# The gated unit's second group: four column blocks moved ahead of the first group's last four

## The chip, the cores and the metric

The kernel runs on one core of a Trainium2 chip. The metric is the device time of one launch in microseconds, lower is better. The engines that the text names are PE (TensorE, matmuls), PEld (its weight loads), DVE (VectorE), ACT (ScalarE), POOL (GpSimd) and SP (SyncE, which issues most DMAs). A few tenths of a per cent lie between runs of one kernel.

## The reference

Three stages follow each other on 2304 tokens of width 512 (4 batches of 576 rows, 8 heads of 64):

```
q, k rotated by position; attn = softmax(q k^T / 8);  x = attn v            # per batch and head
e = argmax(x w_gate); y = gate * sigmoid(x w_og)[e] * (relu(x w1[e]) w2[e])  # one of 8 experts, inner width 1024
out = (sigmoid(y Wg) * (y Wv)) Wo                                            # gated unit, inner width 1536
```

The last line is the gated unit. Its three weights come as float64 and the rest as float32; the result must hold to float32.

## The kernel before, in words

**Split matmuls.** Every large matmul works on operands that are split in two, a high half rounded to TensorE's faster fp32r type (`hi`) and a low half with what is left (`lo`), and adds three products: high by high, high by low, low by high. A weight is split by one ScalarE copy (`hi`) and one VectorE subtraction (`lo`).

**Expert stage.** The tokens are sorted by expert and worked in fourteen columns, numbered by their place in the program: a pair column has 256 tokens, a single one 128. Each column has eight units, j = 0 to 7: four for the first expert matrix (`l1`), four for the second (`l2`). In each unit the kernel records that unit's matmuls and the weight split of the unit three places ahead (lines 764 to 776), which also asks for the next column's weights. Column 13 is the held one: its results are scattered to `y_dram` during the gated unit (`put`, lines 868 to 875), in two scatters from POOL's queue.

**Conversion.** TensorE can't use float64, so `conv` (lines 948 to 973) makes a float32 piece from the two 32-bit halves of each number: ScalarE computes `mag` and `rnd`, VectorE the two steps of `sgn`, POOL the sum. There are 36 pieces of 128x512, one of each weight (gate `g`, value `v`, output `o`) for each of the twelve column blocks. Each needs a 512 KB load into one of three `cv` buffers (`conv_load`). Fifteen pieces are converted in the expert stage, at units 1 and 5 of pair columns and at unit 1 of single ones (line 913), from column 3 on. The other 21 are converted in the first group of the gated unit, two in each block (lines 1269 and 1270).

**Gated unit.** The tokens stand in six groups of 384 (`NG`), and the inner width in twelve column blocks of 128 (`NF`). The loop of lines 1263 to 1278 walks over the 72 pairs of group and block. One step records: the gate and value matmuls of this block (`gv`, 24 matmuls into the PSUM tiles `t` and `v`), the sigmoid on ScalarE, the product `gf` on VectorE and its two halves `gh` (ScalarE) and `gl` (POOL); the conversions that are due; the weight splits of the block two steps on (`wsplit`: `gh`, `gl`, `vh`, `vl`, `oh`, `ol`); and the output matmuls of the block before (`om`, 9 matmuls that add into three PSUM banks `o0` to `o2`). The three banks belong to one group at a time. After a group's twelfth block they are copied out (`ob`, two by ScalarE, one by VectorE) and stored. In four of a group's steps the next group's tokens, loaded by `load_y`, are transposed on TensorE and split (`ty`, its low half is `yl`).

Nothing reorders what is recorded: each engine and each DMA queue works in the order of the program, and waits at an instruction until its operands are there.

Of the kernel before, what the change touches and what calls it, by code (L numbers as in the profile page):

```python
# [9 lines left out]
F32 = mybir.dt.float32  # L10
F32R = mybir.dt.float32r
# [4 lines left out]
ALU = mybir.AluOpType  # L16
# [19 lines left out]
MAIN = list(range(NMAIN))  # L36
SPARES = (list(range(NMAIN, NCOL)),)
PAIRS = {*EARLY, *LATE_PAIRS}
HELD = MAIN[-1]
FRONT = 3  # L40
# [5 lines left out]
TG = 384  # L46
NG = NT // TG
KD = DM // 128
NF = FF // 128
# [3 lines left out]
NSPL = 4  # L53
CVB = 3
SCALE = D**-0.5
CONV_RATE = 2
CONV_AT = (1, 5)
TAIL = (3, 3, 0, 8, 9, 9, 9, 9, 9)
HI_EARLY = 6
NXG = 4  # L60
# [4 lines left out]
def tile_kernel(  # L65
# [16 lines left out]
    nc = tc.nc  # L82
    ctx.enter_context(tc.manual_schedule())

    def pool(stack, name, bufs, side="left", space=None):
        kw = {} if space is None else {"space": space}
        return stack.enter_context(tc.tile_pool(name=name, bufs=bufs, side=side, reuse_waits="tile", **kw))
# [622 lines left out]
    M = {}  # L710
# [14 lines left out]
    def tiles(s):  # L725
        return 2 if s in PAIRS else 1
# [9 lines left out]
    def more_ids():  # L736
        while M["ids"] < min(M["want"], len(M["seq"])):
            load_ids(M["seq"][M["ids"]])
            M["ids"] += 1
# [123 lines left out]
    def scale_y(s):  # L863
        for i in range(tiles(s)):
            ysb[s, i] = y = yp.tile([128, 512], F32, tag="ysb", name="ysb")
            nc.vector.tensor_scalar(out=y, in0=yps[s][i], scalar1=sc[s, i], scalar2=None, op0=ALU.mult)
# [10 lines left out]
    def moe_units(seq):  # L877

        m = len(seq)
        order = [(s, j) for s in seq for j in range(NPC)]  # L880
        nsp = [0]

        def ahead(upto):
            while nsp[0] < min(upto, len(order)):
                split(*order[nsp[0]])
                nsp[0] += 1

        yield lambda: ahead(1)
        yield lambda: ahead(2)
        yield lambda: (ahead(LOOK), tx(seq[0]))  # L890
        pos = 0
        for i, s in enumerate(seq):
            for j in range(NPC):
                pos += 1

                def unit(i=i, s=s, j=j, pos=pos):
                    (l1 if j < 4 else l2)(s, j)
                    ahead(pos + LOOK)
                    if j == 0 and i:
                        scale_y(seq[i - 1])  # L900
                        put(seq[i - 1], 0)
                        if M["table"]:
                            M["want"] = i + 4
                            more_ids()
                    if j == 4 and i:
                        put(seq[i - 1], 1)
                    if j == 1 and i + 2 < m and (seq is not MAIN or i + 2 != FRONT):
                        gather(seq[i + 2])
                    if s not in PAIRS and 1 <= j <= 4:
                        th(s, j - 1)  # L910
                    if j == 5 and i + 1 < m:
                        tx(seq[i + 1])
                    if seq is MAIN and FRONT <= i < m - 1 and j in CONV_AT[: tiles(s)]:
                        conv()

                yield unit
# [5 lines left out]
    CONV = [(f, n) for f in range(NF) for n in "gvo"]  # L922
    cl, cd = [0], [0]
# [117 lines left out]
    for t in range(NJ * NPAIR):  # L1041
        g, j = divmod(t, NJ)
# [33 lines left out]
        n = g + 2  # L1076
# [83 lines left out]
    moe_s.close()  # L1160


    ysp = pool(ctx, "ysp", 4, "right")
    wsp = [pool(ctx, "wsp0", 1, "right")]
    ytp = pool(ctx, "ytp", 2, "right")
    wsp += [pool(ctx, f"wsp{i}", 1, "right") for i in (1, 2)]
    osp = pool(ctx, "osp", 3, "right")
    gsp = pool(ctx, "gsp", 3, "right")
    NTT = TG // 128
    ytok, yT, ws, gs, ops_ = {}, {}, {}, {}, {}  # L1170

# [2 lines left out]
    def load_y(gr):  # L1174
        ytok[gr] = []
        for t in range(NTT):
            y = ysp.tile([128, DM], F32, tag="yt", name="yt")
            r0 = GROUPS[gr] * TG + t * 128 + 1
            nc.sync.dma_start(out=y, in_=y_dram[r0 : r0 + 128, :])
            ytok[gr].append(y)  # L1180

    def ty(gr, kk):
        if kk == 0:
            yT[gr] = (
                ytp.tile([128, KD, TG], F32R, tag="yh", name="yh"),
                ytp.tile([128, KD, TG], F32R, tag="yl", name="yl"),
            )
        ps = pst.tile([128, 512], F32, tag="t", name="t")
        for t in range(NTT):
            nc.tensor.transpose(ps[:, 128 * t : 128 * t + 128], ytok[gr][t][:, 128 * kk : 128 * kk + 128], idf)  # L1190
        hi, lo = (t[:, kk, :] for t in yT[gr])
        nc.scalar.copy(out=hi, in_=ps[:, 0:TG])
        nc.vector.tensor_tensor(out=lo, in0=ps[:, 0:TG], in1=hi.bitcast(F32), op=ALU.subtract)

    def wsplit(i):
        f = i % NF
        r = []
        gw, vw, ow = M["gw"], M["vw"], M["ow"]
        to = {nm: [wsp[i % 3].tile([128, 512], F32R, tag=nm + x, name=nm + x) for x in "hl"] for nm in "gvo"}
        for nm, t in (("g", gw[:, :, 128 * f : 128 * f + 128]), ("v", vw[:, :, 128 * f : 128 * f + 128]), ("o", ow[:, f, :])):  # L1200
            hi, lo = to[nm]
            shp = (lambda a: a) if nm == "o" else (lambda a: a.rearrange("p (k f) -> p k f", k=KD))
            nc.scalar.copy(out=shp(hi), in_=t)  # L1203
            nc.vector.tensor_tensor(out=shp(lo), in0=t, in1=shp(hi.bitcast(F32)), op=ALU.subtract)  # L1204
            r.append((hi, lo))
        ws[i] = r

    def gv(gr, f):
        i = gr * NF + f
        yh, yl = yT[gr]  # L1210
        pg = pst.tile([128, 512], F32, tag="t", name="t")
        pv_ = psv.tile([128, 512], F32, tag="v", name="v")
        for ps, (wh, wl) in ((pg, ws[i][0]), (pv_, ws[i][1])):
            for kk in range(KD):
                c = slice(128 * kk, 128 * kk + 128)
                nc.tensor.matmul(ps[:, 0:TG], wh[:, c], yh[:, kk, :], start=(kk == 0), stop=False)  # L1216
                nc.tensor.matmul(ps[:, 0:TG], wh[:, c], yl[:, kk, :], start=False, stop=False)  # L1217
                nc.tensor.matmul(ps[:, 0:TG], wl[:, c], yh[:, kk, :], start=False, stop=(kk == KD - 1))  # L1218
        sg = gsp.tile([128, TG], F32, tag="sg", name="sg")
        nc.scalar.activation(out=sg, in_=pg[:, 0:TG], func=AF.Sigmoid)  # L1220
        gf = gsp.tile([128, TG], F32, tag="gf", name="gf")
        nc.vector.tensor_tensor(out=gf, in0=pv_[:, 0:TG], in1=sg, op=ALU.mult)  # L1222
        gh = gsp.tile([128, TG], F32R, tag="gh", name="gh")
        gl = gsp.tile([128, TG], F32R, tag="gl", name="gl")
        nc.scalar.copy(out=gh, in_=gf)  # L1225
        nc.gpsimd.tensor_tensor(out=gl, in0=gf, in1=gh.bitcast(F32), op=ALU.subtract)  # L1226
        gs[i] = (gh, gl)

    def om(gr, f):
        i = gr * NF + f  # L1230
        if f == 0:
            ops_[gr] = [pso2.tile([128, 512], F32, tag=f"o{t}", name=f"o{t}") for t in range(NTT)]
        gh, gl = gs.pop(i)
        wh, wl = ws.pop(i)[2]
        for t in range(NTT):
            ps = ops_[gr][t]
            c = slice(128 * t, 128 * t + 128)
            nc.tensor.matmul(ps, gh[:, c], wh, start=(f == 0), stop=False)  # L1238
            nc.tensor.matmul(ps, gh[:, c], wl, start=False, stop=False)  # L1239
            nc.tensor.matmul(ps, gl[:, c], wh, start=False, stop=(f == NF - 1))  # L1240
        if f == NF - 1:
            for t in range(NTT):
                o = osp.tile([128, 512], F32, tag="ob", name="ob")
                (nc.vector.tensor_copy if t % 2 else nc.scalar.copy)(o, ops_[gr][t])
                r0 = GROUPS[gr] * TG + t * 128
                nc.sync.dma_start(out=out[r0 : r0 + 128, :], in_=o)

    N = NG * NF
    cd0 = cd[0]
# [10 lines left out]
    psv = pool(ctx, "psv", 2, "right", PSUM)  # L1260
    pso2 = pool(ctx, "pso2", 1, "right", PSUM)
    wsplit(1)
    for i in range(N + 1):
        gr, f = divmod(i, NF)
        if i < N:
            if f == 2 and gr + 1 < NG:
                load_y(gr + 1)
            gv(gr, f)
            while cd[0] < min(len(CONV), max(3 * (i + 3), cd0 + CONV_RATE * (i + 1))):
                conv()  # L1270
            if i + 2 < N:
                wsplit(i + 2)
        if i == 1:
            put(HELD, 1)
        if i >= 1:
            om(*divmod(i - 1, NF))
        if i < N and f >= 7 and f < 11 and gr + 1 < NG:
            ty(gr + 1, f - 7)


def _consts():
# [60 lines left out]
```

## Time and profile before

| | us |
|---|---|
| median of 3 runs | 1140.25 (1137.76 to 1144.18) |
| the profiled execution | 1140.11 |
| its span, first to last instruction | 1138.3 |
| PE busy | 1074.3 (94%) |
| DVE busy | 771.9 (68%) |
| ACT busy | 583.7 (51%) |
| POOL busy | 353.1 (31%) |

The span is what the profiler saw between the first and the last instruction; the execution's own time is 1.8 us more. Attention ends and the experts begin at about 430 us, the gated unit's first matmul starts at 658.85 us. A busy share is an average over these three stages. TensorE's granted clock was 1.00 of full speed in every stretch of the expert stage and the gated unit.

In a row of a timeline the first number is the start in us from the span's start, the second the duration. Instructions of one engine overlap a little at their ends, and a matmul's recorded duration (0.33 us) is longer than the distance to the next one.

### The profile page before, as it was taken

To read this page: it belongs to the slowest core of one execution; us is meant where nothing else is said; L and a number is where in the kernel's file an instruction comes from. 1 tells how busy PE (TensorE), PEld (TensorE's weight loads), DVE (VectorE), ACT (ScalarE), POOL (GpSimd) and SP (SyncE) were. 2 spreads that over 40 slices of the span, in tenths; PEclk is the share of its full clock that TensorE was granted. 3 is DMA by queue.
4 is the path that set the end of the run, shared out by engine and by line. 5 is a ranking of instruction groups with operands and counts; after the bars stand their busy time and mean duration, and the time that the engine had idled before them with its cause. 6 is when DMAs were issued, how large, how long until landed. Compare 5 with 4: busy or idle time off the path is not lost. (4 is left out here: it accounts for less than half of the span.)

```text
span 1138.3 us, 20687 instructions
## 1 busy us (share of the span) xinstructions
PE 1074.3 (94%) x7682; PEld 958.8 (84%) x7682; DVE 771.9 (68%) x1439; ACT 583.7 (51%) x1122; POOL 353.1 (31%) x336
## 2 busy tenths in 40 slices
PE   7799989999988999999999998889999999999998
PEld 6688778878867988888988887689999999999997
DVE  5778787878776886888888778864454444545442
ACT  3456555546554345567567555644443444444442
POOL 6335554654612104333233044521111111111111
PEclk8899999999999999999999999999999999999999
DMA  4134045025008296698999435310010010100000
GB/s 111 37 73 86 7 54 92 19 53 97 21 22 223 46 188 234 210 307 286 308 305 308 148 102 186 112 56 1 1 56 1 1 56 1 56 1 2 28 1 28
DMA packets 97053, 111.61 MB, mean 98 GB/s; under 512 B 16817, under 2 KB 75441, under 8 KB 96946
## 3 DMA queue, kind: packets, MB, share of 16 engines
q1 hardware_dynamic: 92482, 97.81, 30.6%
q0 software_dynamic: 4320, 12.08, 3.6%
q8 instruction: 62, 1.02, 0.4%
q14 instruction: 45, 0.37, 0.1%
q10 hardware_dynamic: 144, 0.33, 0.1%
HBM read 103.03 MB, written 15.56 MB: 104 GB/s over the span
## 5 line engine op out<-in xcount | busy, mean ns | idle before, releaser
L1226 POOL TENSOR_TENSOR gl<-gf,gh 128x384 fp32r<-128x384 f32 x72 | 73.4, 1019 | 349.4 <-ACT gh L1225 349.4
L291 ACT ACTIVATE p<-s,nm 128x576 f32<-128x576 f32 x144 | 105.6, 738 | 123.8 <-DVE nm L284 123.8
L770 DVE TENSOR_TENSOR lo<-wr,hi 128x1024 fp32r<-128x1024 f32 x112 | 150.4, 1359 | 16.8 <-ACT hi L769 15.8
L1222 DVE TENSOR_TENSOR gf<-v,sg 128x384 f32<-128x384 f32 x72 | 40.0, 555 | 136.7 <-PE v L1218 136.7
L284 DVE TENSOR_REDUCE nm<-s 128x1 f32<-128x576 f32 x144 | 102.8, 751 | 38.4 <-PE s L278 25.1
L1204 DVE TENSOR_TENSOR gl<-gw,gh 128x512 fp32r<-128x512 f32 x72 | 73.8, 1025 | 68.9 <-ACT gh L1203 68.9
L1225 ACT CAST gh<-gf 128x384 fp32r<-128x384 f32 x72 | 36.9, 513 | 162.1 <-DVE gf L1222 162.1
L769 ACT CAST hi<-wr 128x1024 fp32r<-128x1024 f32 x106 | 109.5, 1051 | 3.6 <-PE y L860 2.7
L1216 PE MATMUL t<-yh,gh 128*128 128x384 f32 x288 | 98.8, 343 | 9.2 <-ACT sg L1220 8.3
L324 PE MATMUL t<-idf,p 128*128 128x128 f32 x576 | 84.5, 281 | 21.2 <-DVE pt L310 17.6
L1218 PE MATMUL t<-yh,gl 128*128 128x384 f32 x288 | 97.5, 339 | 4.2 <-DVE gl L1204 4.2
L1217 PE MATMUL t<-yl,gh 128*128 128x384 f32 x288 | 96.6, 336 | 0.0
L327 ACT COPY pt<-t 128x512 f32<-128x512 f32 x144 | 79.5, 589 | 33.2 <-PE t L324 26.4
L1216 PE MATMUL v<-yh,vh 128*128 128x384 f32 x288 | 96.2, 334 | 0.0
L1217 PE MATMUL v<-yl,vh 128*128 128x384 f32 x288 | 96.2, 334 | 0.0
L1218 PE MATMUL v<-yh,vl 128*128 128x384 f32 x288 | 96.2, 334 | 0.0
L324 PEld LDWEIGHTS t<-idf,p 128*128 128x128 f32 x576 | 66.6, 145 | 28.2 <-DVE pt L310 22.9
L1240 PE MATMUL o<-oh,gl 128*128 128x512 f32 x216 | 86.2, 399 | 0.2 <-POOL gl L1226 0.2
L1239 PE MATMUL o<-ol,gh 128*128 128x512 f32 x216 | 85.3, 395 | 0.0
L1238 PE MATMUL o<-oh,gh 128*128 128x512 f32 x216 | 84.0, 389 | 0.0
L829 PE MATMUL h<-xh,hi 128*128 128x256 f32 x288 | 82.0, 285 | 1.9 <-DVE hl L834 1.9
L829 PE MATMUL h<-xl,hi 128*128 128x256 f32 x288 | 82.0, 285 | 1.6 <-DVE sc L805 1.6
(227 smaller groups left out, 2900.0 us busy)
## 6 DMA issues: line engine op xcount, KB each, us to landing
wr<-in_moe_w_dram SPq DMA_DIRECT2D x112, 512.0 KB
cv<-in_moe_w_gate_dram SPq DMA_DIRECT2D x12, 512.0 KB
cv<-in_moe_w_val_dram SPq DMA_DIRECT2D x12, 512.0 KB
cv<-in_moe_w_out_dram SPq DMA_DIRECT2D x12, 512.0 KB
yt<-y_dram SPq DMA_DIRECT2D x18, 256.0 KB
out_dram<-ob SPq DMA_DIRECT2D x18, 256.0 KB
kraw<-in_k_dram SPq DMA_DIRECT2D x16, 256.0 KB
qraw<-in_q_dram SPq DMA_DIRECT2D x16, 256.0 KB
```

The source lines that it names most:

```text
L284: nc.vector.tensor_reduce(out=nm, in_=s[:, :, 0:288], axis=AX.XY, op=ALU.max, negate=True)
L291: nc.scalar.activation(out=P[g, j][:, e, :].rearrange("p (a b) -> p a b", a=2), in_=s[:, :, 0:288], func=AF.Exp, bias=nm, scale=1.0, accum ...
L324: nc.tensor.transpose(ps[:, 128 * c : 128 * c + 128], src[:, e, k0 + 128 * c : k0 + 128 * c + 128], idf)
L769: nc.scalar.copy(out=hi, in_=t)
L770: nc.vector.tensor_tensor(out=lo, in0=t, in1=hi.bitcast(F32), op=ALU.subtract)
L829: nc.tensor.matmul(ps[:, c, :], w[:, kk, 128 * c : 128 * c + 128], x[:, kk, :], start=first, stop=last)
L1216: nc.tensor.matmul(ps[:, 0:TG], wh[:, c], yh[:, kk, :], start=(kk == 0), stop=False)
L1217: nc.tensor.matmul(ps[:, 0:TG], wh[:, c], yl[:, kk, :], start=False, stop=False)
L1218: nc.tensor.matmul(ps[:, 0:TG], wl[:, c], yh[:, kk, :], start=False, stop=(kk == KD - 1))
L1238: nc.tensor.matmul(ps, gh[:, c], wh, start=(f == 0), stop=False)
L1239: nc.tensor.matmul(ps, gh[:, c], wl, start=False, stop=False)
L1240: nc.tensor.matmul(ps, gl[:, c], wh, start=False, stop=(f == NF - 1))
```

## The change

The loop of the gated unit now follows a list, `ORDER`: blocks 0 to 7 of the first group, blocks 0 to 3 of the second, blocks 8 to 11 of the first, blocks 4 to 11 of the second, then the other groups as before. Since the three banks hold the first group's sums until its last block, the output matmuls of the second group's first eight blocks are put off (the table `AFTER`): they follow from step 16 on, two in a step until they have caught up. The products of the four early blocks wait in a pool of their own (`ghd`). The output weights of the second group's blocks 0 to 7 are not split with their gate and value weights but by `late_w`, two output blocks ahead, into the tiles that the conversion used (`mag` and `rnd` of the pool `cvt`).

Pair columns of the expert stage get a third conversion, at unit 3 (`CONV_AT`), so that 20 pieces are done by its end and 16 are left. These are spread over twelve steps by the table `CONV_BY`. The second group's tokens are loaded at step 0 and transposed in steps 3 to 6. The pool `ysp` has three buffers instead of four, `sg` and `gf` have two instead of three.

```diff
-CONV_RATE = 2
-CONV_AT = (1, 5)
+CONV_BY = (1, 3, 4, 6, 7, 9, 10, 12, 13, 14, 15, 16)
+ND = 4
+CONV_AT = (1, 3, 5)
...
-                    if seq is MAIN and FRONT <= i < m - 1 and j in CONV_AT[: tiles(s)]:
+                    if seq is MAIN and FRONT <= i < m - 1 and j in CONV_AT[: 3 if s in PAIRS else 1]:
                         conv()
...
+    LATE, LATE_O = ([(1, f) for f in range(n)] for n in (ND, 2 * ND))
+    ORDER = [(0, f) for f in range(NF - ND)] + LATE
+    ORDER += [(0, f) for f in range(NF - ND, NF)] + [(1, f) for f in range(ND, NF)]
+    ORDER += [(gr, f) for gr in range(2, NG) for f in range(NF)]
+    AFTER = {i: [] for i in range(len(ORDER) + 1)}
+    for i, x in enumerate(ORDER):
+        if x[0] != 1:
+            AFTER[i + 1].append(x)
+    for f in range(NF):
+        AFTER[NF + ND + (f + 1) // 2 if f < 2 * ND else NF + f + 1].append((1, f))
...
     def wsplit(i):
+        gr, f = ORDER[i]
+        ws[gr, f] = [wsplit_one(wsp[i % 3], nm, f) for nm in ("gv" if (gr, f) in LATE_O else "gvo")]
...
-        wh, wl = ws.pop(i)[2]
+        wh, wl = wod_[i] if i in LATE_O else ws.pop(i)[2]
...
+    def late_w(f):
+        wod_[1, f] = wsplit_one(M["cvt"], "o", f, ("mag", "rnd"))
+
     for i in range(N + 1):
-        gr, f = divmod(i, NF)
         if i < N:
-            if f == 2 and gr + 1 < NG:
+            gr, f = ORDER[i]
+            if i == 0:
+                load_y(1)
+            elif f == 2 and 1 <= gr < NG - 1:
                 load_y(gr + 1)
             gv(gr, f)
-            while cd[0] < min(len(CONV), max(3 * (i + 3), cd0 + CONV_RATE * (i + 1))):
+            ready = 3 * (ORDER[min(i + 3, N - 1)][1] + 1)
+            while cd[0] < min(len(CONV), max(ready, cd0 + CONV_BY[min(i, len(CONV_BY) - 1)])):
                 conv()
             if i + 2 < N:
                 wsplit(i + 2)
         if i == 1:
             put(HELD, 1)
-        if i >= 1:
-            om(*divmod(i - 1, NF))
-        if i < N and f >= 7 and f < 11 and gr + 1 < NG:
-            ty(gr + 1, f - 7)
+        for x in AFTER[i]:
+            om(*x)
+            if x in LATE_O[:-2]:
+                late_w(x[1] + 2)
+        if i in (NF, NF + 2):
+            late_w((i - NF) // 2)
+        if i < N:
+            if gr == 0 and 3 <= f < 7:
+                ty(1, f - 3)
+            elif 1 <= gr < NG - 1 and 7 <= f < 11:
+                ty(gr + 1, f - 7)
```

Where the instructions now stand, at three places. In a row, the first names are the tile written and the tiles read. Line numbers of the changed kernel differ from those before.

On VectorE, in the gated unit's first group, a step before the change (step 2) begins with the product of its block and has two conversions (four rows of `sgn`) ahead of three weight splits:

```order
L1222 TENSOR_TENSOR gf<-v,sg 128x384
L961 TENSOR_SCALAR sgn<-cv 128x512
L962 SCALAR_TENSOR_TENSOR sgn<-mag,sgn 128x512
L961 TENSOR_SCALAR sgn<-cv 128x512
L962 SCALAR_TENSOR_TENSOR sgn<-mag,sgn 128x512
L1204 TENSOR_TENSOR gl<-gw,gh 128x512
L1204 TENSOR_TENSOR vl<-vw,vh 128x512
L1204 TENSOR_TENSOR ol<-ow,oh 128x512
```

Steps 8 and 9 after the change, the first two of the second group's early blocks:

```order
L1237 TENSOR_TENSOR gf<-v,sg 128x384
L962 TENSOR_SCALAR sgn<-cv 128x512
L963 SCALAR_TENSOR_TENSOR sgn<-mag,sgn 128x512
L1216 TENSOR_TENSOR gl<-gw,gh 128x512
L1216 TENSOR_TENSOR vl<-vw,vh 128x512
L1237 TENSOR_TENSOR gf<-v,sg 128x384
L962 TENSOR_SCALAR sgn<-cv 128x512
L963 SCALAR_TENSOR_TENSOR sgn<-mag,sgn 128x512
L1216 TENSOR_TENSOR gl<-gw,gh 128x512
L1216 TENSOR_TENSOR vl<-vw,vh 128x512
```

One conversion stands in each of these steps, and no split of output weights.

On VectorE in the expert stage, a pair column from its second unit to the end of its sixth, before the change (`hl` is the low half of the hidden values, `lo` that of a weight piece, `xl` that of the next column's tokens):

```order
L770 TENSOR_TENSOR lo<-wr_4837,hi 128x1024
L961 TENSOR_SCALAR sgn<-cv 128x512
L962 SCALAR_TENSOR_TENSOR sgn<-mag,sgn 128x512
L834 SCALAR_TENSOR_TENSOR hl<-h,hh 128x512
L770 TENSOR_TENSOR lo<-wr_4838,hi 128x1024
L834 SCALAR_TENSOR_TENSOR hl<-h,hh 128x512
L770 TENSOR_TENSOR lo<-wr_4839,hi 128x1024
L770 TENSOR_TENSOR lo<-wr_4840,hi 128x1024
L770 TENSOR_TENSOR lo<-wr_4833,hi 128x1024
L802 TENSOR_TENSOR xl<-t,xh 128x4x128
```

The same stretch after the change:

```order
L771 TENSOR_TENSOR lo<-wr_4837,hi 128x1024
L962 TENSOR_SCALAR sgn<-cv 128x512
L963 SCALAR_TENSOR_TENSOR sgn<-mag,sgn 128x512
L835 SCALAR_TENSOR_TENSOR hl<-h,hh 128x512
L771 TENSOR_TENSOR lo<-wr_4838,hi 128x1024
L835 SCALAR_TENSOR_TENSOR hl<-h,hh 128x512
L771 TENSOR_TENSOR lo<-wr_4839,hi 128x1024
L962 TENSOR_SCALAR sgn<-cv 128x512
L963 SCALAR_TENSOR_TENSOR sgn<-mag,sgn 128x512
L771 TENSOR_TENSOR lo<-wr_4840,hi 128x1024
L771 TENSOR_TENSOR lo<-wr_4833,hi 128x1024
L803 TENSOR_TENSOR xl<-t,xh 128x4x128
```

The third conversion stands between the splits of the seventh and the eighth piece.

On TensorE, where the first group ends, before the change: the last output matmuls of the group (`o_10887` is its third bank), and behind them the next block's gate matmuls:

```order
L1238 MATMUL o_10887<-oh,gh 128x512
L1239 MATMUL o_10887<-ol,gh 128x512
L1240 MATMUL o_10887<-oh,gl 128x512
L1216 MATMUL t<-yh,gh 128x384
L1217 MATMUL t<-yl,gh 128x384
L1218 MATMUL t<-yh,gl 128x384
```

After the change (`o_10939` is the third bank, `o_11885` the first one as the second group uses it; `mag` and `rnd` now hold its output weights):

```order
L1254 MATMUL o_10939<-oh,gh 128x512
L1255 MATMUL o_10939<-ol,gh 128x512
L1256 MATMUL o_10939<-oh,gl 128x512
L1254 MATMUL o_11885<-mag,gh 128x512
L1255 MATMUL o_11885<-rnd,gh 128x512
L1256 MATMUL o_11885<-mag,gl 128x512
```

The second group's output matmuls follow the first group's without a block between them.

## Rows read from the trace of the kernel before

**Rows 1.** The page's first line.

```profile
span 1138.3 us, 20687 instructions
```

**Rows 2.** Timeline of PE: start us, us, engine, line, operation, tiles [idle before].

```profile
658.85 0.45 PE L1216 MATMUL t<-yh,gh 128*128 128x384 f32 x1
...
663.15 0.33 PE L1216 MATMUL t<-yh,gh 128*128 128x384 f32 x1
...
750.65 0.33 PE L1216 MATMUL t<-yh,gh 128*128 128x384 f32 x1
...
751.00 0.34 PE L1218 MATMUL t<-yh,gl 128*128 128x384 f32 x1
...
756.69 0.39 PE L1240 MATMUL o<-oh,gl 128*128 128x512 f32 x1
756.92 0.33 PE L1216 MATMUL t<-yh,gh 128*128 128x384 f32 x1
```

**Rows 3.** Timeline of ACT, two sigmoids while the third group's tokens are transposed.

```profile
810.04 0.49 ACT L1220 ACTIVATE sg<-t 128x384 f32<-128x384 f32 x1 [1.41 <-PE t L1218]
...
816.62 0.49 ACT L1220 ACTIVATE sg<-t 128x384 f32<-128x384 f32 x1 [1.42 <-PE t L1218]
```

**Rows 4.** Waits of PE in the first group: total us, times, longest us.

```profile
PE t L1216 <- ACT sg L1220: 4.8, 2, 3.5
PE t L1218 <- DVE gl L1204: 4.2, 6, 1.0
```

**Rows 5.** Windows, first group: us, busy of PE, PEld, DVE, ACT, POOL, clock, DMA, GB/s.

```profile
658.85:750.65 91.80, 78.28 (x400) 68.87 (x400) 78.87 (x99) 56.57 (x109) 44.65 (x35) 1.00 0.38 118
```

**Rows 6.** Timeline of DVE: the first product, and one whole step.

```profile
663.41 0.56 DVE L1222 TENSOR_TENSOR gf<-v,sg 128x384 f32<-128x384 f32 x1 [0.25 <-PE v L1218]
...
694.44 0.55 DVE L1222 TENSOR_TENSOR gf<-v,sg 128x384 f32<-128x384 f32 x1
694.91 0.41 DVE L961 TENSOR_SCALAR sgn<-cv 128x512 uint32<-128x512 uint32 x1
696.14 1.11 DVE L962 SCALAR_TENSOR_TENSOR sgn<-mag,sgn 128x512 uint32<-128x512 uint32 x1 [0.82 <-ACT mag L959]
697.17 0.41 DVE L961 TENSOR_SCALAR sgn<-cv 128x512 uint32<-128x512 uint32 x1
697.69 1.60 DVE L962 SCALAR_TENSOR_TENSOR sgn<-mag,sgn 128x512 uint32<-128x512 uint32 x1
699.22 0.68 DVE L1204 TENSOR_TENSOR gl<-gw,gh 128x512 fp32r<-128x512 f32 x1
699.82 1.77 DVE L1204 TENSOR_TENSOR vl<-vw,vh 128x512 fp32r<-128x512 f32 x1
701.51 0.68 DVE L1204 TENSOR_TENSOR ol<-ow,oh 128x512 fp32r<-128x512 f32 x1
702.12 0.54 DVE L1222 TENSOR_TENSOR gf<-v,sg 128x384 f32<-128x384 f32 x1
```

**Rows 7.** Timelines of POOL, SP and ACT around the second group's token loads.

```profile
677.72 1.26 POOL L870 DMA_INDIRECT y_dram<-ysb,idt  x1 [0.15 <-issue]
...
680.95 1.29 SPq L1179 DMA_DIRECT2D yt<-y_dram  x3
...
689.46 0.69 ACT L959 ACTIVATE mag<-cv 128x512 f32<-128x512 f32 x1 [0.18 <-DMA cv<-in_moe_w_val_dram]
```

**Rows 8.** Timeline of DVE, the copy of the first group's second bank.

```profile
759.05 0.68 DVE L1244 COPY ob<-o 128x512 f32<-128x512 f32 x1
```

**Rows 9.** Timeline of DVE in a pair column of the expert stage.

```profile
512.84 2.86 DVE L770 TENSOR_TENSOR lo<-wr,hi 128x1024 fp32r<-128x1024 f32 x1
...
516.22 3.48 DVE L770 TENSOR_TENSOR lo<-wr,hi 128x1024 fp32r<-128x1024 f32 x3
```

**Rows 10.** Windows, two pair columns with two conversions each; columns as in rows 5.

```profile
463.79:486.68 22.89, 22.89 (x150) 20.92 (x148) 18.69 (x21) 12.89 (x17) 8.01 (x6) 1.00 0.78 262
501.82:525.29 23.47, 23.15 (x149) 20.91 (x148) 20.16 (x23) 12.90 (x17) 6.06 (x5) 1.00 0.94 320
```

More of the change, by code (lines that the diff above doesn't have):

```diff
@@ L1160, in tile_kernel @@
     moe_s.close()
-    ysp = pool(ctx, "ysp", 4, "right")
+    ysp = pool(ctx, "ysp", 3, "right")
     wsp = [pool(ctx, "wsp0", 1, "right")]
@@ L1168, in tile_kernel @@
     gsp = pool(ctx, "gsp", 3, "right")
+    gsp2 = pool(ctx, "gsp2", 2, "right")
+    ghd = pool(ctx, "ghd", ND, "right")
     NTT = TG // 128
@@ L1193, in ty, with wsplit_one @@
         nc.vector.tensor_tensor(out=lo, in0=ps[:, 0:TG], in1=hi.bitcast(F32), op=ALU.subtract)
-    def wsplit(i):
[L1196 to L1206, printed above, removed]
+    LATE, LATE_O = ([(1, f) for f in range(n)] for n in (ND, 2 * ND))
[8 more added lines that the diff above has]
+        AFTER[NF + ND + (f + 1) // 2 if f < 2 * ND else NF + f + 1].append((1, f))
+    def wsplit_one(pl, nm, f, tags=None):
+        t = M["ow"][:, f, :] if nm == "o" else M[nm + "w"][:, :, 128 * f : 128 * f + 128]
+        shp = (lambda a: a) if nm == "o" else (lambda a: a.rearrange("p (k f) -> p k f", k=KD))
+        hi, lo = (pl.tile([128, 512], F32R, tag=t, name=t) for t in tags or (nm + "h", nm + "l"))
+        nc.scalar.copy(out=shp(hi), in_=t)
+        nc.vector.tensor_tensor(out=shp(lo), in0=t, in1=shp(hi.bitcast(F32)), op=ALU.subtract)
+        return hi, lo
+    def wsplit(i):
+        gr, f = ORDER[i]
+        ws[gr, f] = [wsplit_one(wsp[i % 3], nm, f) for nm in ("gv" if (gr, f) in LATE_O else "gvo")]
     def gv(gr, f):
-        i = gr * NF + f
+        i = gr, f
         yh, yl = yT[gr]
@@ L1218, in gv @@
                 nc.tensor.matmul(ps[:, 0:TG], wl[:, c], yh[:, kk, :], start=False, stop=(kk == KD - 1))
-        sg = gsp.tile([128, TG], F32, tag="sg", name="sg")
+        sg = gsp2.tile([128, TG], F32, tag="sg", name="sg")
         nc.scalar.activation(out=sg, in_=pg[:, 0:TG], func=AF.Sigmoid)
-        gf = gsp.tile([128, TG], F32, tag="gf", name="gf")
+        gf = gsp2.tile([128, TG], F32, tag="gf", name="gf")
         nc.vector.tensor_tensor(out=gf, in0=pv_[:, 0:TG], in1=sg, op=ALU.mult)
-        gh = gsp.tile([128, TG], F32R, tag="gh", name="gh")
-        gl = gsp.tile([128, TG], F32R, tag="gl", name="gl")
+        pl = ghd if (gr, f) in LATE else gsp
+        gh = pl.tile([128, TG], F32R, tag="gh", name="gh")
+        gl = pl.tile([128, TG], F32R, tag="gl", name="gl")
         nc.scalar.copy(out=gh, in_=gf)
@@ L1229, in om @@
     def om(gr, f):
-        i = gr * NF + f
+        i = gr, f
         if f == 0:
@@ L1262, in tile_kernel @@
     wsplit(1)
+    wod_ = {}
+    def late_w(f):
+        wod_[1, f] = wsplit_one(M["cvt"], "o", f, ("mag", "rnd"))
     for i in range(N + 1):
-        gr, f = divmod(i, NF)
         if i < N:
-            if f == 2 and gr + 1 < NG:
+            gr, f = ORDER[i]
+            if i == 0:
+                load_y(1)
+            elif f == 2 and 1 <= gr < NG - 1:
                 load_y(gr + 1)
             gv(gr, f)
-            while cd[0] < min(len(CONV), max(3 * (i + 3), cd0 + CONV_RATE * (i + 1))):
+            ready = 3 * (ORDER[min(i + 3, N - 1)][1] + 1)
+            while cd[0] < min(len(CONV), max(ready, cd0 + CONV_BY[min(i, len(CONV_BY) - 1)])):
                 conv()
```

## The prediction

> **What bounds the kernel now.** I read the span first [rows 1] and then looked for the place where the critical chain leaves TensorE. From 750.65 us on it stays on TensorE almost to the end, one column block of the gated unit every 6.27 us (750.65 to 756.92) [rows 2], or 6.58 us where the transposes of the next group's tokens are in it (810.04 to 816.62) [rows 3]. The first group is different. Its twelve blocks run from 658.85 to 750.65 us, 91.8 us [rows 2]. Their matmuls would need: the first block, which has no output matmuls yet, 4.3 us (658.85 to 663.15); seven at 6.27; four with transposes at 6.58; together 74.5 us. So this one group loses **17.3 us**, and that is the most that the change can take back there.
>
> Who holds TensorE up? Its recorded waits in the group end with the sigmoid on ScalarE (4.8 us) and with the low half of the gate weights on VectorE (4.2 us) [rows 4]; the rest of the loss lies between matmuls, as matmul ends are modelled. Over the stretch VectorE is busy 78.87 of 91.80 us [rows 5]. One block's work on VectorE shows why [rows 6]: the product gf at 694.44, two weight conversions (two instructions each), the splits gl, vl, ol, and the next gf at 702.12. That is 7.68 us per block against the 6.27 us of TensorE. Two things stretch it: 0.82 us of waiting for ScalarE's mag, and the blocks in which a POOL addition runs beside a VectorE instruction with two SBUF inputs (sgn 1.60 and vl 1.77, where ol takes 0.68). The bound of the first group is VectorE's conversion work.
>
> **The change part by part.**
>
> *Fewer conversions, over more blocks.* Five conversions move into the expert stage; 16 instead of 21 remain, and they are spread over twelve steps (1, 2, 1, 2, 1, 2, 1, 2, 1, 1, 1, 1) before sixteen blocks are due, since four blocks of the second group come ahead of the first group's last four. A step with one conversion lacks the stretch from 697.17 to 699.22, which is 2.05 us: 7.68 - 2.05 = 5.63 us [rows 6]. The four steps 6 to 9 split no output weights: 0.60 us less each (ol to gf, 701.51 to 702.12). The transposes of the second group now lie in steps 3 to 6, with one yl each, taken as 0.54 us like gf, which has the same shape.
>
> VectorE starts on step 0 at 663.41 us, with the first block's gf [rows 6]. To the end of step 10 it needs 4 x 7.68 + 7 x 5.63 - 4 x 0.60 + 4 x 0.54 = 30.7 + 39.4 - 2.4 + 2.2 = 69.9 us, so to 733.3; in step 11 the gate split is done after 5.63 - 2.30 (vl and ol follow it, 699.82 to 702.12) = 3.3 us, at 736.6. That split is what block 13 needs. TensorE would be there earlier: nine output matmuls at 0.23 us (756.69 to 756.92) [rows 2] are 2.1 us, so a block without them is 6.27 - 2.1 = 4.2 us, and four such blocks stand in a row (steps 9 to 12, since the second group's output matmuls must wait for the first group's banks). 4.3 + 4 x 6.27 + 4 x 6.58 + 4 x 4.2 = 72.5 us after 658.85 is 731.35, and the low half is first used 0.35 us into a block (751.00). **VectorE is 4.9 us late** there, in stalls that begin in the light steps. After step 11 no conversion is left, blocks cost TensorE 6.27 again, and VectorE catches up. Bounds: 0, if the 0.82 us wait for mag hides when there is one conversion (eight steps by 0.82 is 6.6 us, more than the lateness); 7, if the first conversion's sgn takes the 1.60 us of the second instead of 1.11 (eight by 0.5, less what overlaps). I take 4.9, since the row for it is the same block of the same stage.
>
> *The wait for the weights' DMA.* In the old order the loads of the second group's tokens stand behind the second scatter of the held column (issued 677.72); SyncE waits with them to 680.95, three weight loads queue behind, and ScalarE's mag starts only at 689.46 [rows 7]. It is inside the 17.3 us. Now these loads stand right behind those of the first group and wait for the first scatter, which is released as the first block begins. With the same 3.2 us from scatter to loads (677.72 to 680.95) they go out by 666.4 even if that scatter came as late as 663.15, and the weight load behind them is needed in the second conversion of step 1, which begins some 2 us after 663.41 + 5.63 = 669. I cost it at nothing; if that cover is gone, it is the old step's excess once more, some 2 us.
>
> *The group boundary.* The last output matmuls of the first group and the first of the second now stand next to each other, in step 16. Before, a whole block lay between, which hid the copying out of the three banks. There the matmuls ended at 756.92 while VectorE copied its bank at 759.05, or 758.45 without the ol split (0.60 us) that the new step lacks [rows 2, 8]. Its copy ends 0.68 us later, at 759.13; TensorE has 0.70 us (three matmuls) on the first bank meanwhile: 759.13 - 756.92 - 0.70 = **1.5 us** of stall, once. Bounds 0.9, if VectorE's vl split has also moved ahead by its 0.6 us, and 2.1, if the ol split's time isn't saved.
>
> *Late output weights.* Eight splits move from the weight pool to the conversion's tiles; their number stays. In steps 17 to 19 TensorE has two output blocks beside its gate and value matmuls, 8.4 us a step, and the other engines one split more than in an ordinary block. A late split waits for the output block two before it and takes about 1.4 us (0.68 as ol [rows 6], and ScalarE's copy taken as long); between the two lie 2.1 us of another output block at the least, and 4.2 us of gate and value matmuls. Behind the waiting ScalarE copy stand only the sigmoid and copies of a block that isn't finished. Cost nothing; without the cover, some 1 us for each of a few.
>
> *The third conversion in the expert stage.* Five pair columns get one at their fourth unit. Alone it costs VectorE 1.1 us (0.41 and, taken as ol, which has the same shape and no POOL work beside it, 0.68) [rows 6], and POOL's addition beside the next weight split makes that 2.86 us instead of 1.2 [rows 9]: 2.75 us together. Two conversions are free today: in the pair column from 463.79 TensorE is busy 22.89 of 22.89 us. VectorE is idle 4.2 us in that column and 3.3 us in the tighter one from 501.82 [rows 10], more than 2.75, and splits run up to three units ahead. The DMA share there is 0.94, at 320 GB/s, so one more 512 KB load (1.6 us at that rate) fits but narrowly. Bounds 0 and 5 x 2.75 = 13.8 us; I take **0.5 us** for all five, near the lower end, since the column with two shows nothing.
>
> **Sum** on the profiled execution, which took 1140.11 us beside its span of 1138.3 (the median of the runs is 1140.25, the same for this purpose): 1140.1 - 17.3 + 4.9 + 1.5 + 0.5 = **1129.7 us**, 0.9% less.
>
> **The rivals.**
>
> *Clean.* With one conversion in a step, VectorE's pauses fall into time that TensorE leaves, and its lateness is 0 to 1 us: 1140.1 - 17.3 + 0.5 + 1.5 = 1124.8. For it: lateness is counted at one point, and only if the mag wait stays in each step. Against it: the mag wait stands in every step of the old group.
>
> *Half given back.* One-conversion steps take 0.3 us longer than worked out (2.4 us over eight), and each third conversion delays its column by the 1.1 us of its own two instructions (5.6 us): 1140.1 - 17.3 + 7.3 + 1.5 + 5.6 = 1137.2. For it: VectorE's idle time of 3.3 us in a pair column [rows 10] is little more than the 2.75 us that the conversion takes.
>
> *Slower: the expert stage pays in full.* The place is unit 3 of the five pair columns. ScalarE's mag (0.69) [rows 7] and rnd, taken as long, and VectorE's 2.75 us come one behind the other in front of the next split, 4.1 us each, 20.5 us in all: 1140.1 - 17.3 + 4.9 + 1.5 + 20.5 = 1149.7. It decides from 17.3 - 6.4 = 10.9 us on, 2.2 us a column. Against it: VectorE's idle time in these columns.
> The Trainium skill (SBUF — State Buffer, section Who interferes with whom) says that of a VectorE instruction with two SBUF inputs and a GpSimd one that reads SBUF, whichever starts second waits for the whole of the first. The trace agrees with the block (2.86 against 1.2 us). By this rule POOL would wait if the split came first, the price would be 1.1 + 1.4 us a column, and this rival would end near 1142.
>
> *It doesn't help.* If the serial chain of gf, gh, mag, sgn and split holds each step, and not the amount of work, the steps stay near 7.6 us and the time near 1140. Against it: VectorE's pauses are 0.82 of 7.68 us.
>
> **How the numbers follow.** Forecast 0.60 (its own range 1126 to 1133), clean 0.16, half 0.14, slower 0.05, no help 0.05. 0.5% is 5.7 us, about what a measurement of this kernel can tell from no change: faster means under 1134.5. That holds for forecast, clean and a little of half (0.04): 0.80; the rest of half and no help: 0.15; slower 0.05. The range runs from the clean case to just past half, 1124 to 1138.
>
> **What the next profile would show.** Right: blocks 0 to 8 without a recorded wait of more than a few tenths, stalls of some 5 us on the gate split in steps 9 to 13, one wait of 1.5 us on the bank copy, pair columns still 23 to 23.5 us long. Wrong: pair columns over 24 us or the single ones behind them longer (the third conversion isn't free); a wait for a cv load in steps 1 to 3; waits on the late splits' halves in steps 17 to 19; or no stall at all in steps 9 to 13 (then 4.9 was too much).

## The result, and the profile after

The changed kernel takes 1129.55 us (median of 5 runs, 1125.84 to 1130.99) against 1140.25 before (1137.76 to 1144.18): ratio 0.9902, 95% interval 0.9873 to 0.9931. The forecast was 1129.7. The profiled execution took 1129.55 us as well, and its span is shorter than the one of [rows 1] by 10.5 us:

```profile
span 1127.8 us, 20456 instructions
PE 1076.3 (95%) x7682; PEld 961.7 (85%) x7682; DVE 771.9 (68%) x1439; ACT 582.2 (52%) x1122; POOL 360.3 (32%) x336
```

The counts of busy instructions are those of before on every engine (the total falls by 231, among instructions that are not counted as busy), and VectorE is busy for the same 771.9 us: work has moved, none has gone.

Where the time came from is read from TensorE's timeline (start, duration, idle time before in brackets). The rows are the first gate matmuls of steps 0, 9, 13, 14, 16, 17 and 24, and, in step 16, the last output matmul of the first group and the first of the second:

```profile
658.54 0.45 PE L1231 MATMUL t<-yh,gh 128*128 128x384 f32 x1
...
714.87 0.33 PE L1231 MATMUL t<-yh,gh 128*128 128x384 f32 x1
...
735.75 0.44 PE L1231 MATMUL t<-yh,gh 128*128 128x384 f32 x1 [0.84 <-ACT gh L1215]
...
742.61 0.33 PE L1231 MATMUL t<-yh,gh 128*128 128x384 f32 x1
...
755.14 0.33 PE L1231 MATMUL t<-yh,gh 128*128 128x384 f32 x1
...
761.17 0.40 PE L1256 MATMUL o<-oh,gl 128*128 128x512 f32 x1
762.30 0.50 PE L1254 MATMUL o<-mag,gh 128*128 128x512 f32 x1 [0.73 <-ACT ob L1260]
...
765.13 0.33 PE L1231 MATMUL t<-yh,gh 128*128 128x384 f32 x1
...
816.54 0.33 PE L1231 MATMUL t<-yh,gh 128*128 128x384 f32 x1
```

Step 24 is the first step whose work is the same in both orders. From step 0 to step 24 it is 816.54 - 658.54 = **158.0 us**. Before, step 24 begins here:

```profile
827.09 0.33 PE L1216 MATMUL t<-yh,gh 128*128 128x384 f32 x1
```

With the start of [rows 2] that is 827.09 - 658.85 = **168.2 us**. So 10.2 of the 10.5 us come from this stretch. This length is the measure for all experiments below. In two profiles of the changed kernel it came out within 0.1 us (158.0 and 157.9). Whole times differ by several us from profile to profile, and much of that lies further ahead: the first expert column with a conversion begins between 432.8 and 440.6 us in the profiles here, and the first gate matmul between 650.6 and 659.9 us.

TensorE's waits from step 0 to step 17, by engine and line waited for (total, times, longest), answer to [rows 4]:

```profile
PE t L1231 <- ACT gh L1215: 1.6, 4, 0.8
PE o L1254 <- ACT ob L1260: 0.7, 1, 0.7
PE o L1254 <- DVE ob L1260: 0.3, 1, 0.3
PE t L1231 <- ACT sg L1235: 0.2, 1, 0.2
PE t L1233 <- DVE gl L1216: 0.2, 1, 0.2
```

They sum to 3.0 us. In [rows 4] the window ends at 744.30 us, just ahead of the third and last long wait for a sigmoid; over the whole first group of the kernel before, the first of its two rows reads

```profile
PE t L1216 <- ACT sg L1220: 8.3, 3, 3.5
```

so there the two rows are 8.3 + 4.2 = 12.5 us, not 9.0. Two kinds are left after the change: the weight splits of the light steps (steps 9 to 12, which have no output matmuls), and the copy of the banks, `ob`, which was no wait before.

A light step on VectorE, to be held against [rows 6]:

```profile
724.98 0.69 DVE L1216 TENSOR_TENSOR gl<-gw,gh 128x512 fp32r<-128x512 f32 x1
725.59 1.78 DVE L1216 TENSOR_TENSOR vl<-vw,vh 128x512 fp32r<-128x512 f32 x1
727.29 0.54 DVE L1237 TENSOR_TENSOR gf<-v,sg 128x384 f32<-128x384 f32 x1
727.76 0.41 DVE L962 TENSOR_SCALAR sgn<-cv 128x512 uint32<-128x512 uint32 x1
728.99 1.04 DVE L963 SCALAR_TENSOR_TENSOR sgn<-mag,sgn 128x512 uint32<-128x512 uint32 x1 [0.82 <-ACT mag L960]
730.06 0.69 DVE L1216 TENSOR_TENSOR gl<-gw,gh 128x512 fp32r<-128x512 f32 x1
```

From gl to gl it is 5.08 us; the prediction had 5.63 - 0.60 = 5.03. The 0.82 us wait for `mag` is there in each of the light steps.

The expert stage, windows of the two pair columns of [rows 10] with three conversions instead of two (us, then busy time of PE, PEld, DVE, ACT, POOL):

```profile
463.89:486.78 22.89, 22.89 (x150) 20.92 (x149) 20.13 (x23) 13.92 (x19) 10.43 (x8) 1.00 0.80 270
502.00:525.38 23.38, 23.06 (x150) 20.89 (x149) 21.12 (x25) 13.90 (x19) 8.32 (x6) 1.00 0.95 318
```

Both columns keep their length: TensorE is busy in all of the 22.89 us of the first, as before, and VectorE has 1.0 to 1.4 us more work in each. That is not all that the third conversions cost VectorE. Over the ten columns that hold conversions, before and after:

```profile
440.46:632.12 191.66, 184.36 (x1181) 163.93 (x1180) 161.41 (x193) 125.76 (x185) 61.10 (x44) 1.00 0.83 276
440.58:632.16 191.58, 184.36 (x1181) 163.94 (x1180) 171.16 (x203) 130.84 (x195) 74.65 (x49) 1.00 0.87 289
```

VectorE's busy time grows by 9.75 us, 1.95 for each of the five conversions; a part of it falls into the single columns. The ten columns take 191.6 us, as before.

### The profile page after: what moved, and what is told of

Its sections match the earlier page's. It is cut to its first block, busy times and chain, and to the rows that moved or that the text cites. A ratio compares the mean times of both kernels' runs of the same rounds, so it can differ in the third digit from the quotient of the medians.

```text
span 1127.8 us, 20456 instructions
## 1 busy us (share of the span) xinstructions
PE 1076.3 (95%) x7682; PEld 961.7 (85%) x7682; DVE 771.9 (68%) x1439; ACT 582.2 (52%) x1122; POOL 360.3 (32%) x336
## 5 line engine op out<-in xcount | busy, mean ns | idle before, releaser
L771 DVE TENSOR_TENSOR lo<-wr,hi 128x1024 fp32r<-128x1024 f32 x112 | 156.4, 1409 | 14.7 <-ACT hi L770 14.3
L830 PE MATMUL h<-xh,lo 128*128 128x256 f32 x288 | 81.5, 283 | 0.0
L1235 ACT ACTIVATE sg<-t 128x384 f32<-128x384 f32 x72 | 35.3, 491 | 81.8 <-PE t L1233 81.8
L861 PE MATMUL y<-hi,hl 128*128 128x512 f32 x184 | 73.0, 397 | 4.6 <-DVE hl L847 4.4
```

The lines of the kernel that those rows point to most:

```text
L771: nc.vector.tensor_tensor(out=lo, in0=t, in1=hi.bitcast(F32), op=ALU.subtract)
L830: nc.tensor.matmul(ps[:, c, :], w[:, kk, 128 * c : 128 * c + 128], x[:, kk, :], start=first, stop=last)
L861: nc.tensor.matmul(ps, hl, rh, start=False, stop=False)
```

## The experiments

Ten edited kernels ran, and the changed kernel once more, each timed beside the kernel before. The kernel before took 1133.87, 1137.31 and 1138.23 us (medians) beside the three sets, so times are compared as ratios, and the stretch from step 0 to step 24 across all of them. The first four test where the gain comes from.

**The third conversion alone.** The kernel before with this edit:

```diff
-CONV_RATE = 2
-CONV_AT = (1, 5)
+CONV_BY = (2, 4, 6, 7, 9, 10, 12, 13, 15, 16)
+CONV_AT = (1, 3, 5)
...
```

> The kernel before with the third conversion in the five pair columns alone: the blocks stay in their old order, and the 16 conversions left are spread over the first ten steps (2,2,2,1,2,1,2,1,2,1). Theory A (the loss is VectorE's work, counted step by step): six steps of 7.68 and four of 5.63 us and three yl of 0.54 are 70.2 us; from 663.4 less the 2.3 us of vl and ol the gate split of block 11 is done at 731.3, TensorE wants it at 727.4, so 3.9 us are lost instead of 17.3, plus 1 to 2 us for the weight load's wait that stays: 1128 to 1129 us, as fast as the changed kernel without any reordering. Theory B (the reordered blocks make the room): not more than about half of the gain, 1135 us.

Measured: ratio 0.9910 (0.9889 to 0.9932), the changed kernel's own ratio within the intervals. Its first gate matmul and that of step 24:

```profile
651.21 0.44 PE L1216 MATMUL t<-yh,gh 128*128 128x384 f32 x1
...
809.50 0.33 PE L1216 MATMUL t<-yh,gh 128*128 128x384 f32 x1
```

158.3 us, against 158.0 for the changed kernel. **The conversions moved into the expert stage give the whole gain; the reordered blocks aren't needed for it.** The size was off: 7.3 us are lost in the first group where 5 to 6 were expected.

**The reordered blocks alone.** The changed kernel with the old conversions in the expert stage:

```diff
-CONV_BY = (1, 3, 4, 6, 7, 9, 10, 12, 13, 14, 15, 16)
-CONV_AT = (1, 3, 5)
+CONV_BY = (2, 4, 6, 8, 9, 11, 13, 15, 17, 19, 20, 21)
+CONV_AT = (1, 5)
...
```

> The changed kernel without the third conversion in the pair columns: the reordered blocks alone, with 21 conversions over twelve steps (2,2,2,2,1,2,2,2,2,2,1,1). Theory A: to the end of step 10 VectorE needs nine steps of 7.68 and two of 5.63, 80.2 us, and is 15.2 us late at block 13, with 1.6 us at the bank copy: 17.3 become 16.8, 1139 to 1140 us, no gain. Theory B: the reordered blocks are what gains, 1131 to 1134 us.

Measured: ratio 0.9988 (0.9975 to 1.0001).

```profile
651.40 0.44 PE L1231 MATMUL t<-yh,gh 128*128 128x384 f32 x1
...
818.92 0.33 PE L1231 MATMUL t<-yh,gh 128*128 128x384 f32 x1
```

167.5 us: 0.7 less than before. Theory A holds, theory B falls. The count by steps came out too: step 14 begins at 745.0 us, so steps 0 to 13 take 93.6 us, 14.8 more than the 78.8 that TensorE needs, where 15.2 were expected. The four early blocks let the last conversions come two steps later (step 11 instead of 9), but they bring four blocks' weight splits with them and no output matmuls, so VectorE wins next to no room.

**The early token loads alone.** In the kernel before, `load_y(1)` at step 0 as the change has it.

> The kernel before with one line changed: the second group's tokens are loaded at step 0 instead of step 2, so that the weight loads don't queue behind the wait for the second scatter. Theory A: VectorE saves the 1.3 us that it idled for the late weight load, 1138.5 to 1139.5 us. Theory C (the wait of the weight loads was the larger part of the loss): 1132 us or less.

Measured: ratio 0.9988 (0.9975 to 1.0001).

```profile
651.58 0.44 PE L1216 MATMUL t<-yh,gh 128*128 128x384 f32 x1
...
820.52 0.33 PE L1216 MATMUL t<-yh,gh 128*128 128x384 f32 x1
```

168.9 us, no shorter than the 168.2 of before. Theory C falls. The ratio hints at a gain of about 0.1%, its interval reaches to no gain at all, and the stretch shows none; that is left open.

**Who sets the light steps.** The recorded waits there name ScalarE's `gh`. The changed kernel without four low halves of value weights, in the splits of `ORDER[10]` to `ORDER[13]`; the high half stands in their place:

```diff
...
+        if nm == "v" and skip:
+            return hi, hi
         nc.vector.tensor_tensor(out=shp(lo), in0=t, in1=shp(hi.bitcast(F32)), op=ALU.subtract)
...
+        ws[gr, f] = [wsplit_one(wsp[i % 3], nm, f, None, 10 <= i <= 13) for nm in ("gv" if (gr, f) in LATE_O else "gvo")]
```

> The changed kernel without the low half of the value weights in the four splits of steps 8 to 11 (the high half is used in its place, so these blocks are computed wrongly): VectorE loses four instructions of 1.77 us, ScalarE none. Theory A (VectorE's work sets the light steps of 5.06 to 5.67 us): they fall to 4.2 to 4.4 us, 4 us less in all, 1125 to 1126 us. Theory D (ScalarE's chain of gh, mag, rnd and the high split sets them, as the recorded waits for gh say): nothing changes, 1129 to 1130 us.

Measured: ratio 0.9878 (0.9856 to 0.9900). Steps 0, 9, 13 and 24 begin at

```profile
650.58 0.44 PE L1233 MATMUL t<-yh,gh 128*128 128x384 f32 x1
...
706.86 0.33 PE L1233 MATMUL t<-yh,gh 128*128 128x384 f32 x1
...
724.91 0.34 PE L1233 MATMUL t<-yh,gh 128*128 128x384 f32 x1
...
805.43 0.33 PE L1233 MATMUL t<-yh,gh 128*128 128x384 f32 x1
```

so steps 9 to 12 take 18.05 us where the changed kernel takes 735.75 - 714.87 = 20.88. Together with step 13 and the steps up to 24 the stretch is 154.9, 3.1 us less, without a change to ScalarE's work. So ScalarE's chain alone doesn't set these steps: its `gh` comes late because it stands behind `mag`, which stands behind the copy of `gf`, which VectorE is late with. Theory D falls. VectorE's 0.82 us of waiting for `mag` is a part of the same loop in each step; what a shorter chain on ScalarE would give wasn't run. 4 us were expected: step 9 stays at 5.08 us, since the gate split for which step 10 waits stands ahead of the first instruction taken away.

The other seven look for a better version and for the end of the expert stage's room.

**The changed kernel again**, on one chip with the next three.

> The changed kernel once more, to stand on the same chip as the three that follow: a ratio near 0.990 to the kernel before.

Measured: ratio 0.9915 (0.9895 to 0.9934).

**Three more conversions, in the held column** (column 13, which had none), with the reordered blocks:

```diff
-CONV_BY = (1, 3, 4, 6, 7, 9, 10, 12, 13, 14, 15, 16)
+CONV_BY = (1, 2, 4, 5, 7, 8, 10, 11, 12, 13)
...
-                    if seq is MAIN and FRONT <= i < m - 1 and ...
+                    if seq is MAIN and FRONT <= i < m and ...
```

> The changed kernel with three more conversions in the held pair column (its units 1, 3 and 5; VectorE is busy 14.2 of 23.0 us there), so that 13 are left: 1,1,2,1,2,1,2,1,1,1 in steps 0 to 9 and none in steps 10 and 11. Theory A (VectorE's work in the gated unit is what the time follows): the held column keeps its length, the light steps 9 to 13 lose 4 to 4.7 us of their 4.75 us of stall, 0.986 to the kernel before. Theory E (a conversion moved into the expert stage is paid there): the held column grows by 2 to 3 us a conversion, 0.990 or more.

Measured: ratio 0.9911 (0.9892 to 0.9929), no better than the changed kernel beside it, and not the 0.986 of theory A. The stretch falls to 154.8 us (813.90 - 659.11), 3.2 less, and steps 9 to 12 to 4.2 to 4.5 us each, as theory A says; but from the held column to the gated unit it is 30.1 us where the changed kernel has 26.4, so the expert stage takes as much back.

**The same with the old order of the blocks.** The kernel of the first experiment, with the held column and `CONV_BY = (1, 3, 4, 5, 7, 8, 10, 11, 13)`:

> The same eight further conversions in the expert stage (five pair columns, three in the held one) with the blocks in their old order, 13 left over nine steps (1,2,1,1,2,1,2,1,2). Theory A: VectorE needs 58.9 us for these steps and is level with TensorE at block 10, so 0.5 to 2 us are lost instead of 17.3, and there is no stall at the bank copy: 0.986, no slower than the same with the reordered blocks. Theory B (the reordered blocks make room): slower than the reordered one by 3 us or more, 0.989.

Measured: ratio 0.9891 (0.9874 to 0.9909). Its held column begins, and its gated unit and step 24:

```profile
627.82 0.28 PE L829 MATMUL h<-xh,hi 128*128 128x256 f32 x1
...
657.94 0.69 PE L1216 MATMUL t<-yh,gh 128*128 128x384 f32 x1
...
811.36 0.33 PE L1216 MATMUL t<-yh,gh 128*128 128x384 f32 x1
```

The stretch is 153.4 us, shorter than with the reordered blocks, and theory B falls again; the 0.986 of theory A is missed by the same 3.7 us as above. From the held column to the gated unit it is 30.1 us, where the changed kernel has 658.54 - 632.16 = 26.4:

```profile
632.16 0.28 PE L830 MATMUL h<-xh,hi 128*128 128x256 f32 x1
```

What TensorE waits for there, in the kernel with the held conversions:

```profile
PE t L1190 <- DMA yt<-y_dram: 3.9, 3, 1.9
```

It is the load of the first group's tokens. SyncE issues it 22.3 us after the held column's start, where it was 18.4 in the changed kernel; no wait for a weight split of the held column is recorded there.

**The bank copy covered.** The reordered kernel with the held conversions, and the second group's output blocks 0 and 2 one step later (0 in step 17, 2 in step 18):

```diff
-        AFTER[NF + ND + (f + 1) // 2 if f < 2 * ND else NF + f + 1].append((1, f))
+        AFTER[17 if f < 2 else 18 if f < 5 else 19 if f < 7 else 20 if f < 8 else NF + f + 1].append((1, f))
```

> The reordered kernel with the three held conversions, and the second group's first output block moved behind the next block's gate and value matmuls (the output blocks 0 and 1 in step 17, 2 to 4 in step 18, 5 and 6 in step 19, 7 in step 20), so that the copy of the banks is covered. Theory A (the 1.63 us of step 16 is the bank copy, nothing else): step 16 falls to 6.3 us and the three output blocks of step 18 wait for no late split, 1.6 us less than without this move, 0.985. Otherwise the wait reappears at the late splits in step 18, and the time stays.

Measured: ratio 0.9891 (0.9872 to 0.9909). Step 16 is 6.27 us, without a stall. Step 18 with its three output blocks is 11.06, where 6.27 and two more of 2.1 make 10.5: a stall of some 0.6 us comes back there, 0.3 of it recorded at the low half of a late split, `rnd`. The stretch is 153.7 us (813.58 - 659.85), 1.1 less than without the edit, not 1.6, and the ratio is not the 0.985 of the full gain.

**The held conversions in its first units**, 0, 1 and 2, with the old order:

> The kernel with the old block order and eight further conversions, with the three of the held column moved from its units 1, 3 and 5 to its units 0, 1 and 2. Theory G (the held column grew by 3.7 us because its last conversion keeps VectorE from the branch behind the expert stage, for which the loads of the first group's tokens wait): the stretch from the held column to the gated unit falls back from 30.1 to 26.4 us, the first step from 5.6 to 4.3, and the ratio to the kernel before is 0.985 to 0.987. Otherwise (the conversions themselves take the time): it stays near 0.989.

Measured: ratio 0.9852 (0.9825 to 0.9879).

```profile
626.41 0.28 PE L829 MATMUL h<-xh,hi 128*128 128x256 f32 x1
...
654.23 0.44 PE L1216 MATMUL t<-yh,gh 128*128 128x384 f32 x1
...
806.32 0.33 PE L1216 MATMUL t<-yh,gh 128*128 128x384 f32 x1
```

From the held column to the gated unit it is 27.8 us, 2.3 less, and the wait for the tokens has shrunk:

```profile
PE t L1190 <- DMA yt<-y_dram: 1.3, 1, 1.3
```

So the place of the conversions counts, as theory G says; 1.4 of the 3.7 us stay. That VectorE's late arrival at the branch is the way by which it acts was argued, not shown: the weight loads in SyncE's queue moved too.

**The same conversions with the reordered blocks and the covered bank copy:**

> The same eight conversions and held units 0, 1 and 2 with the reordered blocks and the second group's first output block one step later. Theory A (only the count of conversions and their spread matter, not the order of the blocks): equal to the one with the old order within 1.5 us, 0.985 to 0.987. Theory B: faster than it by 3 us or more.

Measured: ratio 0.9835 (0.9810 to 0.9859). The stretch is 152.6 us (808.51 - 655.89), against 152.1 with the old order; the ratios' intervals overlap. Again the order of the blocks makes no difference that shows. Both beat the kernel before by about 1.5%. The interval of this one lies below those of the changed kernel, which begin at 0.9873 and 0.9895; that of the old order reaches to 0.9879.

**A fourth conversion in the pair columns**, at unit 7, in the changed kernel (`CONV_AT = (1, 3, 5, 7)`, 11 left):

> The changed kernel with a fourth conversion in the five pair columns, at their eighth unit; 11 are left for ten steps of the gated unit. Theory A: the light steps lose their 4.75 us; but VectorE was busy 21.1 of 23.4 us in the tight pair columns, and the conversion at unit 7 stands just ahead of the single column's first splits, whose lead is 0.4 to 1.9 us: 1 to 2.5 us more for each of the four single columns behind a pair, 4 to 10 us, so 0.989 to 0.995 to the kernel before. Otherwise (the expert stage still has room): 0.986.

Measured: ratio 0.9854 (0.9826 to 0.9882). My expectation failed. A pair column, and the two single columns that grew, of the four behind a pair that were to suffer:

```profile
482.81:498.07 15.26, 13.79 (x90) 11.88 (x88) 15.05 (x20) 12.25 (x20) 9.14 (x6) 1.00 1.00 343
498.07:521.54 23.47, 23.15 (x149) 20.91 (x148) 21.19 (x25) 15.06 (x21) 8.47 (x7) 1.00 0.96 330
598.76:614.07 15.31, 13.59 (x86) 11.44 (x84) 14.54 (x18) 11.78 (x19) 7.68 (x7) 1.00 0.96 317
```

The same single columns of the changed kernel:

```profile
486.78:501.92 15.14, 13.80 (x89) 11.89 (x88) 14.11 (x18) 12.25 (x20) 6.83 (x5) 1.00 1.01 334
602.62:617.22 14.60, 13.49 (x86) 11.39 (x84) 12.79 (x16) 11.80 (x19) 6.62 (x6) 1.00 0.92 288
```

The pair column keeps its 23.5 us, the single ones grow by 0.1 and 0.7 us, and the other single columns stay as they were. The stretch falls by 5.5 us to 152.5 (807.51 - 655.05). The expert stage still has room for a fourth conversion at the end of each pair column, although in the first single column above, where its work falls, VectorE is now busy for 15.05 of 15.26 us.

## Why the prediction was right, step by step

| step of the prediction | predicted us | measured us |
|---|---|---|
| VectorE late at block 13 | 4.9 | 5.3 |
| bank copy in step 16 | 1.5 | 1.6 |
| third conversion, five columns | 0.5 | 0 |
| wait for the weights' DMA | 0 | 0 |
| late splits in steps 17 to 19 | 0 | 0 |

The total came out within 0.2 us of the forecast, while the runs spread over 5 us: that closeness is luck. The terms are a better test, and they hold within 0.5 us each.

*VectorE's lateness.* Steps 0 to 13 take 742.61 - 658.54 = 84.1 us. By the prediction's own count TensorE needs 72.5 up to block 13 and 6.27 for it, 78.8, so 5.3 are lost. The count by steps was sound: the light steps came out at 5.1 us each, and the stalls begin where it says. One thing it did not foresee: step 6 takes 7.06 instead of 6.58 us (a wait of 0.2 for the sigmoid is recorded), so about 0.5 of the 5.3 is lost ahead of the light steps.

*The bank copy.* Step 16 takes 765.13 - 755.14 = 9.99 us; a step and one more output block are 6.27 + 2.1 = 8.4. The prediction named VectorE's copy of the second bank, and that sets the end of the stall:

```profile
762.89 0.68 DVE L1260 COPY ob<-o 128x512 f32<-128x512 f32 x1
...
763.62 0.50 PE L1254 MATMUL o<-mag,gh 128*128 128x512 f32 x1 [0.35 <-DVE ob L1260]
```

The wait for ScalarE's copy of the first bank (0.73 us recorded), which it did not name, falls into the same time.

*The third conversion.* It cost TensorE nothing. Its price on VectorE was mis-sized: 2.75 us were counted, one POOL block of 1.66 included, and 1.95 were added for each conversion over the ten columns. The weight splits `lo` of these columns took 115.1 us instead of 109.2, so an added POOL addition lengthened them by 1.2 us on average and not by a whole further block. The rival that let the expert stage pay in full rested on that price, and the fourth conversion shows that one more would have cost 0.8 us in all.

*What was right in sum but not in cause.* The prediction put the gain down to fewer conversions *over more blocks*, and treated the two as one term. They are not: fewer conversions alone give 158.3 us, more blocks alone 167.5, both 158.0. The same count by steps would have shown it beforehand: it gave 3.9 us of lateness for the old order with 16 conversions and 15.2 for the new one with 21, and it was made only for the experiments. For the old order it came out too small (7.3 us lost, of which 1 to 2 had been set down to a late weight load besides). Its steps 9 and 10 take 7.26 and 8.50 us where TensorE needs 6.58; there a piece is converted just ahead of the split that reads it, and the count has no term for ScalarE, VectorE and POOL one behind the other. In step 10 the trace shows that chain: ScalarE's split waits for POOL's addition, the sigmoid stands behind it, and TensorE waits for the sigmoid:

```profile
725.26 0.62 ACT L1203 CAST oh<-ow 128x512 fp32r<-128x512 f32 x1 [1.38 <-POOL ow L966]
...
726.71 0.44 PE L1216 MATMUL t<-yh,gh 128*128 128x384 f32 x1 [1.55 <-ACT sg L1220]
```

How much of the 7.3 us it makes was not tested by itself. The kernel before has the same chain, and larger:

```profile
742.86 0.62 ACT L1203 CAST oh<-ow 128x512 fp32r<-128x512 f32 x1 [1.65 <-POOL ow L966]
...
744.30 0.44 PE L1216 MATMUL t<-yh,gh 128*128 128x384 f32 x1 [3.53 <-ACT sg L1220]
```

So "the bound of the first group is VectorE's conversion work" was not the whole of it: steps 8 to 10 take 29.9 us there where TensorE needs 19.7 (step 9 has three conversions, not two, and the steps behind it none), and ScalarE waits 5.0 us for POOL in the group. The prediction read 4.8 us of waits for the sigmoid, from a window without the last of them; they are 8.3. With the reordered blocks, in the changed kernel and with the blocks reordered alone, ScalarE has no such wait recorded from step 0 to step 13. That is what the reordering does take away; net of its own splits in the light steps, the 0.7 us of the reordered blocks alone are left.

## What to carry to other kernels

Where one engine's side work holds up a stage, count that work step by step against the bounding engine's steps, for each part of a change by itself: here a reordering that brought its own side work along made little room, while moving work into a stage with idle time gave nearly all of it. The idle engine of the neighbouring stage could be filled nearly to the end (15.05 of 15.26 us) while that column grew by 0.1 us and another by 0.7; the limit is found by adding until the columns grow by more than the addition saves. Where one engine prepares a piece just ahead of another's use of it, a count of one engine's work comes out too small. For changes of a per cent, measure the affected stretch between two fixed instructions in the profile: here it came out within 0.1 us in two profiles of one kernel, while whole times spread by several.

## What the runs showed of the hardware that was not expected

A recorded wait named ScalarE (`gh`, 1.6 us) where taking four 1.8 us instructions away from VectorE alone shortened the steps by 3.1 us in all: here the last engine to signal was not the one that set the pace by itself, since both stand in one chain. And the price of an added conversion beside POOL could not be read from the column that holds it: VectorE's busy time grew by 1.0 to 1.4 us in the two pair columns shown, by 1.95 for each conversion over all ten columns, and the instruction rows before suggested up to 2.75.
